# Attention feeding a soft mixture of experts on one core: small load buffers, repeated-column constants, and the last five weight halves streamed in by rows

## The chip, the cores and the metric

The kernel runs on one core of one Trainium2 chip. The metric is the device time of one execution in microseconds (us), taken as the median of three runs. One further execution was recorded by the hardware profiler; durations of single instructions come from that one.

## The reference, cut to what matters

```python
# q, k, v: (8, 12, 448, 64); phi: (768, 32); w1: (8, 768, 1024); w2: (8, 1024, 768), all float32
scores = q @ k.T / 8                                  # per batch and head
m = max(scores, -1);  e = exp(scores - m)
attn = e / (sum(e, -1) + exp(-m) + 1e-9)
x = (attn @ v) with heads side by side                # (8*448, 768)

logits = x @ phi                                      # (3584, 32): 8 experts of 4 slots
d = exp(logits - max over tokens);  d /= sum over tokens
slot_input = d.T @ x                                  # (32, 768)
h = relu(slot_input[e] @ w1[e]);  slot_out = h @ w2[e]    # per expert, its 4 slots
c = exp(logits - max over slots);  c /= sum over slots
out = c @ slot_out                                    # (3584, 768), written as float32
```

All 3584 tokens must have gone into `slot_input` before any expert can start, and all experts must be done before any output can be written.

## The kernel before, in words

The work has three stages.

**Attention.** The 96 heads are taken as 48 pairs (`NPAIR`), and three pairs make a group (`NP = 3`, 16 groups, two groups per batch). A hand-written loop over `s` from 0 to 48 sets the order of every engine. Step `s` does the second score pass (`Bk`, L298 and L300, with the exponential on ScalarE, L303) of pair `s`, the attention-times-values products (`AV`, L328) of pairs `s` and `s-1`, the transposes (`T`, L204) of pair `s+6`, and the first score pass (`A`, L226 and L235, with the row maximum on VectorE, L230 and L237) of pairs further on. The maxima of a group are negated and put in order by GpSimd (`W1`, L244), and turned by TensorE (`W2`, L264) with ScalarE's copy and exponential (`W3`). In `Bk` the matmul of L300 adds the negated maximum to the scores; its stationary operand is a slice of `sel`, a 0/1 selector whose 128 columns are equal. `N1`/`N2` normalise a pair (the GpSimd part is L353, L358, L359), `PX` (L371, L374) turns it, and once per batch the steps of `P(b)` add that batch to the running logits and `slot_input` sums; two of them use `ones` as stationary operand (L424 and L451). Five of `P(b)`'s pieces for the last batch run after the loop.

**Experts.** `hidden` (L631), `turn` (L638) and `slots` (L647) run for experts 0 to 3 and then for 4 to 7. `slots` walks over the eight rows `kt` of its four `w2` halves.

**Output.** Eight blocks, one per batch: matmul (L690), scaling on ScalarE and VectorE (L696, L698), and output DMAs from SyncE (L702, L703).

**Loads.** Every input DMA is issued by GpSimd and converts float32 to bfloat16 on its way. GpSimd's queue is in order, so the issues stand between its `N2`, `V` and `W1` work. `load(g, nm)` brings q, k or v of a group: q and k in one DMA each, v in two. `V(g)` (L309 to L312) copies v into the layout that `AV` reads. The sixteen weight halves (`halves`: `w1` of experts 0 to 7 are numbers 0 to 7, `w2` of experts 0 to 7 are numbers 8 to 15) are 1536 KB each in bfloat16. A half of `w2` has 8 rows; a row is 128 partitions of 768 numbers, 192 KB. `load_part(i, z0, z1)` brings rows `z0` to `z1` of half `i`.

**Memory.** Before, q, k and v of a group share one of two buffers of the pool `pnat`, each as large as a weight half. Ten halves have buffers of their own (`wpool`). Halves 10 and 11 take the `pnat` buffers when these are free at the end, and 12 to 15 lie over `R`, one large tile that holds attention's working buffers (`qk` for transposed pairs, `x0`/`x1` for a batch's attention output, `wm`, `vp0`/`vp1` for v, `e1`/`e2` for exponentials, `xT`). A row of a late half can be loaded when the buffers under it have been read for the last time. The last ones to come free are `xT`, which is read by the last logits matmuls (L397), and `x1`, which is read by the last `slot_input` matmuls (L451).

Of the kernel before, what the change touches and what calls it, by code (L numbers as in the profile page):

```python
# [23 lines left out]
HG = 6  # L24
NP = 3
W65 = 65
VS = 66
# [3 lines left out]
def kernel(  # L31
# [29 lines left out]
    keep = ctx.enter_context(tc.tile_pool(name="keep", bufs=1))  # L61
    pnat = ctx.enter_context(tc.tile_pool(name="pnat", bufs=2))
    wpool = ctx.enter_context(tc.tile_pool(name="wpool", bufs=10))

# [14 lines left out]

    NQK, NE, VPN = 7, 5, HG * 4 * VS  # L80
# [35 lines left out]
    w_tile = lambda: wpool.tile([128, KC * F], BF16, tag="w", name="w_sb")  # L116
    late0 = [0, KC * F, 2 * KC * F, at_["x1"]]
    for i in range(4):
        w_view(12 + i, R[:, late0[i]:late0[i] + KC * F])

    with ExitStack() as at:
# [10 lines left out]
        def load(g, nm, l0=0, l1=NP):  # L132


            b, h0 = g // 2, (g % 2) * HG
            if g not in nat:
                nat[g] = pnat.tile([128, KC * F], BF16, tag="nat", name="nat")
            z = "qkv".index(nm) * NP * S
            src = {"q": q, "k": k, "v": v}[nm][b, h0:h0 + HG]
            if nm != "v":  # L140
                t = nat[g][:, z:z + NP * S].rearrange("p (l x) -> p l x", l=NP)
                x = src.rearrange("(l h) (j t) d -> (h j) l (t d)", h=2, t=7)
                gdma(out=t[:, l0:l1, :], in_=x[:, l0:l1, :])
            else:
                t = nat[g][:, z:z + HG * 4 * D].rearrange("p (h t d) -> p h t d", h=HG, t=4)
# [19 lines left out]
        for base in (0, 64):  # L165

            nc.gpsimd.affine_select(
                out=sel[base:base + 64], in_=sel[base:base + 64], fill=1.0,
                compare_op=ALU.not_equal, base=0,
                pattern=[[-1, HG], [0, 128]], channel_multiplier=1)  # L170
        nc.vector.memset(halfm, 0.0)
# [108 lines left out]
        def Bk(n, i):  # L280
            g, pl = divmod(n, NP)
            t = qkT[n]
            rs = [slice(0, 64), slice(64, 128)]
            if i < 3:
                pss = [pb_("ps_b") for _ in range(2)]
                outs = [p[:, 0:S] for p in pss]
                cols = slice(i * 128, (i + 1) * 128)
                e = e2_t[st["e2"] % NE]
                st["e2"] += 1
                es = [e[:, hl, :] for hl in range(2)]  # L290
            else:
                pss = [pb_("ps_b")]
                outs = [pss[0][r, 0:S] for r in rs]
                cols = slice(384, 448)
                es = [e1_t]
            m = cols.stop - cols.start
            for hl in range(2):
                nc.tensor.matmul(outs[hl], t[rs[hl], 1, cols], t[rs[hl], 0, :], start=True, stop=False)  # L298
            for hl in range(2):
                nc.tensor.matmul(outs[hl], sel[rs[hl], 2 * pl + hl, 0:m], mT[mg(n)][rs[hl], :],  # L300
                                 start=False, stop=True)
# [82 lines left out]
        def P(b):  # L384
# [37 lines left out]
            def s_max():  # L422
                ps = pa([128, 128], F32, "ps_bc")
                nc.tensor.matmul(ps, ones, v["diag"], start=True, stop=True)  # L424
# [19 lines left out]
            def s_mm():  # L444
                ps = pa([128, KC + 1, NS], F32, "ps_s")
                for j in range(KC + 1):
                    for i in range(4):

                        r = slice(0, 64 if j == KC and i == 3 else 128)
                        w = x[:, i, j * 128:(j + 1) * 128] if j < KC else ones[r]  # L450
                        nc.tensor.matmul(ps[:, j, :], w, v["cd"][r, 4 + i, :], start=(i == 0), stop=(i == 3))  # L451
# [74 lines left out]
        As(1)  # L526
        for nm in "qkv":
# [80 lines left out]
        nc.vector.reduce_max(fold, ident.rearrange("p (i s) -> p s i", i=4), axis=AX.X)  # L608
# [4 lines left out]
        for g in range(2):  # L613
# [27 lines left out]
        def slots(g):  # L641
            pss = [pb_("ps_so") for _ in range(2)]
            order = list(range(FK)) if g == 0 else [4, 5, 6, 7, 0, 1, 2, 3]
            for kt in order:
                for half in range(2):
                    for i in range(4):
                        nc.tensor.matmul(pss[half][32 * i:32 * i + 32, 0:ND],  # L647
                                         hT[g][:, kt, 32 * i:32 * i + 32],
                                         w_sb["w2", 4 * g + i][:, kt, half * ND:(half + 1) * ND],
                                         start=(kt == order[0]), stop=(kt == order[-1]),  # L650
                                         skip_group_check=True)
# [82 lines left out]
```

## Time and profile before

| what | value |
|---|---|
| median of 3 runs | 344.83 us (344.19 to 344.89) |
| profiled execution, whole | 343.46 us |
| its span, first to last instruction | 341.7 us |
| mean granted TensorE clock in it | 0.936 |
| busy in the span: PE, DVE, ACT, POOL | 293.2, 264.6, 253.3, 200.2 us |
| moved by the GpSimd DMA queue | 42.52 MB, its packets taking 80.6% of 16 engines' span |
| moved by the output queue | 11.01 MB |
| read from memory, written to memory | 85.03 MB, 11.01 MB |

PE is TensorE's matmuls, PEld its weight loads (which overlap the matmuls), DVE VectorE, ACT ScalarE, POOL GpSimd, SP SyncE. A line such as L451 is a line of the kernel. In a table row, "idle before" is the time that the engine stood still ahead of those instructions, with what ended the wait behind the arrow. The three stages in this execution: attention to about 275 us, the last batch's sums and the experts to about 301 us, the output from there to the end.

### The profile page before, as it was taken

To read this page: it belongs to the slowest core of one execution; us is meant where nothing else is said; L and a number is where in the kernel's file an instruction comes from. 1 tells how busy PE (TensorE), PEld (TensorE's weight loads), DVE (VectorE), ACT (ScalarE), POOL (GpSimd) and SP (SyncE) were. 2 spreads that over 40 slices of the span, in tenths; PEclk is the share of its full clock that TensorE was granted. 3 is DMA by queue.
4 is the path that set the end of the run, shared out by engine and by line. 5 is a ranking of instruction groups with operands and counts; after the bars stand their busy time and mean duration, and the time that the engine had idled before them with its cause. 6 is when DMAs were issued, how large, how long until landed. Compare 5 with 4: busy or idle time off the path is not lost.

```text
span 341.7 us, 12065 instructions
## 1 busy us (share of the span) xinstructions
PE 293.2 (86%) x5040; PEld 167.2 (49%) x5040; DVE 264.6 (77%) x609; ACT 253.3 (74%) x547; POOL 200.2 (59%) x398
## 2 busy tenths in 40 slices
PE   3898999999999999999999999999998849677700
PEld 1344565656565655656555656565654534321100
DVE  5799999989998999898999999998984553056510
ACT  2476799998999899899989998999799823055500
POOL 8962777958687776678777867687567241000000
PEclk9999999999999999999999999999999978985555
DMA  7990999946999999199999946999919999939996
GB/s 92 126 173 0 172 169 157 197 67 87 189 169 180 134 180 138 24 142 182 161 186 136 195 56 84 156 179 194 181 28 187 154 210 211 169 89 275 338 348 238
DMA packets 42854, 54.30 MB, mean 159 GB/s; under 512 B 2736, under 2 KB 35504, under 8 KB 41904
## 3 DMA queue, kind: packets, MB, share of 16 engines
q0 software_dynamic: 41360, 42.52, 80.6%
q1 hardware_dynamic: 1440, 11.01, 9.9%
q8 instruction: 39, 0.64, 0.7%
q14 instruction: 15, 0.12, 0.1%
HBM read 85.03 MB, written 11.01 MB: 281 GB/s over the span
## 4 chain that ended last, share of the span: by engine, by line
PE 40%; DVE 25%; ACT 13%; issue 8%; DMA 5%; POOL 3%; DVEq 0%; POOLq 0%; ACTq 0%
DVE mx L230 15%; PE ps_av L328 9%; PE ps_b L298 7%; PE ps_a L226 6%; ACT R L303 6%; DMA R<-in_moe_w_dram 5%; PE ps_b L300 5%; PE ps_t L204 4%; PE ps_o L690 3%; ACT R L207 3%; ACT o_sb L696 2%; ACT R L374 2%; DVE mx L237 2%; PE ps_s L451 2%; PE ps_a L235 1%
## 5 line engine op out<-in xcount | busy, mean ns | idle before, releaser
L230 DVE TENSOR_REDUCE mx<-ps_a 128x1 f32<-128x448 f32 x288 | 160.8, 615 | 11.1 <-PE ps_a L226 9.9
L303 ACT ACTIVATE R<-ps_b 128x448 bf16<-128x448 f32 x336 | 158.0, 557 | 13.7 <-PE ps_b L300 9.1
L298 PE MATMUL ps_b<-R 64*128 64x448 bf16 (+1 forms) x384 | 82.3, 357 | 1.0 <-ACT R L374 0.3
L300 PE MATMUL ps_b<-mT,sel 64*128 64x448 bf16 (+1 forms) x384 | 78.2, 352 | 0.0
L226 PE MATMUL ps_a<-R 64*128 64x448 bf16 x288 | 68.5, 364 | 6.0 <-DVE mx L230 4.4
L353 POOL TENSOR_TENSOR R<-ubuf,rec 128x384 bf16<-128x384 f32 x44 | 36.2, 823 | 52.0 <-DVE rec L350 49.9
L328 PE MATMUL ps_av<-R 128*128 128x65 bf16 (+1 forms) x1536 | 64.5, 196 | 1.5 <-DVE ubuf L340 1.4
L328 PEld LDWEIGHTS <-R 128*128 128x128 bf16 (+1 forms) x1536 | 50.3, 100 | 28.1 <-issue 24.1
L204 PEld LDWEIGHTS <-nat 64*64 64x64 bf16 x1344 | 30.1, 113 | 18.9 <-issue 8.6
L374 ACT CAST R<-ps_x 128x512 bf16<-128x512 f32 x47 | 28.1, 598 | 13.8 <-PE ps_x L371 13.8
L204 PE MATMUL ps_t<-ident,nat 64*64 64x64 bf16 x1344 | 30.7, 196 | 7.1 <-DMA nat<-in_q_dram 4.3
L298 PEld LDWEIGHTS <-R 64*128 64x128 bf16 (+1 forms) x384 | 19.2, 97 | 27.9 <-issue 23.1
L300 PEld LDWEIGHTS <-sel 64*128 64x128 bf16 (+1 forms) x384 | 21.0, 97 | 23.1 <-issue 15.8
L237 DVE TENSOR_REDUCE mx<-ps_a 128x1 f32<-128x448 f32 x48 | 29.8, 620 | 0.8 <-PE ps_a L235 0.5
L207 ACT COPY R<-ps_t 128x896 bf16<-128x896 bf16 x20 | 18.4, 919 | 10.6 <-PE ps_t L204 10.6
L340 ACT COPY ubuf<-ps_av 128x455 f32<-128x455 f32 x44 | 24.7, 561 | 2.0 <-PE ps_av L328 1.0
L226 PEld LDWEIGHTS <-R 64*128 64x128 bf16 x288 | 17.8, 94 | 14.4 <-issue 3.6
L690 PE MATMUL ps_o<-w_sb,cT 32*128 32x384 bf16 x64 | 17.6, 456 | 5.9 <-ACT o_sb L696 5.2
L698 DVE TENSOR_SCALAR o_sb<-ps_o,crec 128x768 f32<-128x768 f32 (+1 forms) x16 | 15.5, 1009 | 9.0 <-PE ps_o L690 9.0
L696 ACT ACTIVATE o_sb<-ps_o,crec 128x768 f32<-128x768 f32 x16 | 13.5, 896 | 11.0 <-PE ps_o L690 11.0
L359 POOL TENSOR_TENSOR R<-ubuf,rec 128x128 bf16<-128x128 f32 x44 | 17.5, 398 | 3.7
L371 PE MATMUL ps_x<-ident,R 128*128 128x128 bf16 x192 | 18.8, 219 | 0.3 <-DVE R L359 0.3
(117 smaller groups left out, 371.0 us busy)
## 6 DMA issues: line engine op xcount, KB each, us to landing
w_sb<-in_moe_w_dram POOLq DMA_DIRECT2D x20, 768.0 KB, 9.6
nat<-in_v_dram POOLq DMA_DIRECT2D x32, 192.0 KB, 4.4
out_dram<-o_sb SPq DMA_DIRECT2D x7, 768.0 KB, 8.8
nat<-in_q_dram POOLq DMA_DIRECT2D x15, 336.0 KB, 5.6
nat<-in_k_dram POOLq DMA_DIRECT2D x15, 336.0 KB, 6.5
out_dram<-o_sb SPq DMA_DIRECT2D x7, 576.0 KB, 8.1
nat<-in_moe_w_dram POOLq DMA_DIRECT2D x4, 768.0 KB, 9.8
R<-in_moe_w_dram POOLq DMA_DIRECT2D x4, 384.0 KB, 12.5
```

The costliest lines, as they stand in the source:

```text
L204: nc.tensor.transpose(ps[r, a, c:c + 64], src[r, pl, tok * D:(tok + 1) * D], ident[r, r])
L207: nc.scalar.copy(t, ps)
L226: nc.tensor.matmul(pss[hl][:, 0:S], t[r, 0, i * 128:(i + 1) * 128], t[r, 1, :], start=True, stop=True)
L230: nc.vector.reduce_max(mx[g][:, c:c + 1], pss[hl][:, 0:S], axis=AX.X)
L237: nc.vector.reduce_max(mx[g][:, c:c + 1], ps[:, 0:S], axis=AX.X)
L298: nc.tensor.matmul(outs[hl], t[rs[hl], 1, cols], t[rs[hl], 0, :], start=True, stop=False)
L300: nc.tensor.matmul(outs[hl], sel[rs[hl], 2 * pl + hl, 0:m], mT[mg(n)][rs[hl], :], start=False, stop=True)
L303: nc.scalar.activation(e, p[:, 0:S], AF.Exp, scale=scale)
L328: nc.tensor.matmul(o, eT[n, i, hl][:, qc], vp[g % 2][:, 2 * pl + hl, i, 0:W65], start=(i == 0 and u == 0 and hl == 0), stop=(i == 3), skip ...
L353: eng.tensor_mul(x[:, 0:3, c:c + 128].rearrange("p i (h d) -> p i h d", h=2), u[:, 0:6, 0:D].rearrange("p (i h) d -> p i h d", h=2), rec[: ...
L374: nc.scalar.copy(xT[:, pb, :], ps)
L690: nc.tensor.matmul(pss[i][0:m, half, 0:ND], cT[r, b, 0:m], slot_out[r, half * ND:(half + 1) * ND], start=True, stop=True)
```

## The change

- q, k and v get small buffers inside `R`: `nq0` and `nq1` (q and k of even and odd groups) and one `nv` for v. The pool `pnat` is gone. `R` is ordered anew.
- Because there is one `nv`, v of group `g` is issued right behind `V(g-1)`, in the step where `s` is a multiple of 3, and ahead of q and k of the group after it. Before, it was issued one step later, behind `W1`, and one group further ahead.
- `sel` is one column per head and `ones` one column; the matmuls read them as 128 (or 64) repeated columns, with a step of zero.
- Eleven halves have buffers of their own. They start at steps 1, 4, 7, 10, 13, 16, 22, 25, 28, 31 and 34 (each half in two parts, in that step and the next).
- Halves 11 to 15 lie over `R` from its start, and are loaded by rows from step 38 on.
- `slots` takes its rows in the order 0 to 7 for both expert groups. Before, the second group took 4 to 7 first.

```diff
-    pnat = ctx.enter_context(tc.tile_pool(name="pnat", bufs=2))
-    wpool = ctx.enter_context(tc.tile_pool(name="wpool", bufs=10))
+    wpool = ctx.enter_context(tc.tile_pool(name="wpool", bufs=11))
...
-    ones = const.tile([128, 128], BF16, name="ones")
-    sel = const.tile([128, HG, 128], BF16, name="sel")
+    ones = const.tile([128, 1], BF16, name="ones")
+    sel = const.tile([128, HG], BF16, name="sel")
...
-    sizes = [("qk", NQK * 2 * S), ("x0", 4 * DD), ("wm", 2 * 512), ("vp0", VPN), ("e1", S),
-             ("e2", NE * 2 * S), ("vp1", VPN), ("x1", 4 * DD), ("xT", KC * 512)]
+    sizes = [("nq0", 2 * NP * S), ("nq1", 2 * NP * S), ("nv", NATV), ("wm", 2 * 512),
+             ("qk", NQK * 2 * S), ("vp0", VPN), ("x0", 4 * DD), ("e2", NE * 2 * S), ("e1", S), ("vp1", VPN),
+             ("xT", KC * 512), ("x1", 4 * DD)]
...
-    late0 = [0, KC * F, 2 * KC * F, at_["x1"]]
-    for i in range(4):
-        w_view(12 + i, R[:, late0[i]:late0[i] + KC * F])
+    for i in range(5):
+        w_view(11 + i, R[:, i * KC * F:(i + 1) * KC * F])
...
-                nc.tensor.matmul(outs[hl], sel[rs[hl], 2 * pl + hl, 0:m], mT[mg(n)][rs[hl], :],
+                nc.tensor.matmul(outs[hl], sel[rs[hl], 2 * pl + hl:2 * pl + hl + 1].to_broadcast([64, m]), mT[mg(n)][rs[hl], :],
...
-        half_at = {s: i for i, s in enumerate((1, 4, 10, 13, 16, 22, 25, 28, 34, 37))}
-
-        part_at = {44: ((12, 0, 2), (12, 7, 8)), 45: ((12, 2, 3),), 46: ((12, 3, 4), (13, 0, 7)), 47: ((12, 4, 5),)}
+        half_at = {s: i for i, s in enumerate((1, 4, 7, 10, 13, 16, 22, 25, 28, 31, 34))}
+
+        part_at = {38: ((11, 0, 3),), 41: ((11, 3, 7),), 42: ((11, 7, 8), (12, 0, 1)), 44: ((12, 1, 5),),
+                   45: ((12, 5, 7), (13, 2, 4)), 46: ((12, 7, 8), (13, 4, 8)), 47: ((13, 0, 2), (14, 0, 1))}
...
                 V(g - 2)
+                if s and g - 1 < NG:
+                    load(g - 1, "v")
...
-                if g < NG:
-                    load(g, "v")
+                if s == 1:
+                    load(2, "v")
...
-            if s in (39, 42):
-                i = 10 + (s - 39) // 3
-                load_half(i, 0, pnat.tile([128, KC * F], BF16, tag="nat", name="nat"))
-                load_half(i, 1)
...
-        load_part(12, 5, 7)
-        load_part(13, 7, 8)
-        load_part(14, 0, 8)
+        load_part(14, 1, 8)
+        load_part(15, 0, 1)
...
-        load_part(15, 4, 8)
-        load_part(15, 0, 2)
-        load_part(15, 2, 4)
+        load_part(15, 1, 5)
+        load_part(15, 5, 8)
...
-            order = list(range(FK)) if g == 0 else [4, 5, 6, 7, 0, 1, 2, 3]
-            for kt in order:
+            for kt in range(FK):
```

More of the change, by code (lines that the diff above doesn't have):

```diff
@@ L72 @@
     ident2 = const.tile([128, 128], BF16, name="ident2")
[L73 to L74 removed]
+    ones = const.tile([128, 1], BF16, name="ones")
+    sel = const.tile([128, HG], BF16, name="sel")
     phi_sb = const.tile([128, KC, NS], BF16, name="phi_sb")
     halfm = const.tile([128, 2], F32, name="halfm")
[L80 to L82 removed]
+    NQK, NE, VPN, NATV = 7, 5, HG * 4 * VS, HG * 4 * D
+    sizes = [("nq0", 2 * NP * S), ("nq1", 2 * NP * S), ("nv", NATV), ("wm", 2 * 512),
+             ("qk", NQK * 2 * S), ("vp0", VPN), ("x0", 4 * DD), ("e2", NE * 2 * S), ("e1", S), ("vp1", VPN),
+             ("xT", KC * 512), ("x1", 4 * DD)]
     at_, n_ = {}, 0
@@ L135, in load @@
             b, h0 = g // 2, (g % 2) * HG
-            if g not in nat:
-                nat[g] = pnat.tile([128, KC * F], BF16, tag="nat", name="nat")
-            z = "qkv".index(nm) * NP * S
             src = {"q": q, "k": k, "v": v}[nm][b, h0:h0 + HG]
             if nm != "v":
-                t = nat[g][:, z:z + NP * S].rearrange("p (l x) -> p l x", l=NP)
+                t = part(f"nq{g % 2}", "qk".index(nm) * NP * S, NP * S).rearrange("p (l x) -> p l x", l=NP)
                 x = src.rearrange("(l h) (j t) d -> (h j) l (t d)", h=2, t=7)
@@ L144, in load @@
             else:
-                t = nat[g][:, z:z + HG * 4 * D].rearrange("p (h t d) -> p h t d", h=HG, t=4)
+                t = part("nv", 0, NATV).rearrange("p (h t d) -> p h t d", h=HG, t=4)
                 x = src.rearrange("h (p t) d -> p h t d", t=7)
@@ L169 @@
                 compare_op=ALU.not_equal, base=0,
-                pattern=[[-1, HG], [0, 128]], channel_multiplier=1)
+                pattern=[[-1, HG]], channel_multiplier=1)
         nc.vector.memset(halfm, 0.0)
@@ L423, in s_max @@
                 ps = pa([128, 128], F32, "ps_bc")
-                nc.tensor.matmul(ps, ones, v["diag"], start=True, stop=True)
+                nc.tensor.matmul(ps, ones.to_broadcast([128, 128]), v["diag"], start=True, stop=True)
                 nc.vector.reduce_max(new, ps.rearrange("p (i s) -> p s i", i=4), axis=AX.X)
@@ L449, in s_mm @@
                         r = slice(0, 64 if j == KC and i == 3 else 128)
-                        w = x[:, i, j * 128:(j + 1) * 128] if j < KC else ones[r]
+                        w = x[:, i, j * 128:(j + 1) * 128] if j < KC else ones[r].to_broadcast([r.stop, 128])
                         nc.tensor.matmul(ps[:, j, :], w, v["cd"][r, 4 + i, :], start=(i == 0), stop=(i == 3))
@@ L526 @@
         As(1)
-        for nm in "qkv":
+        for nm in "qk":
             load(2, nm)
-        half_at = {s: i for i, s in enumerate((1, 4, 10, 13, 16, 22, 25, 28, 34, 37))}
-        part_at = {44: ((12, 0, 2), (12, 7, 8)), 45: ((12, 2, 3),), 46: ((12, 3, 4), (13, 0, 7)), 47: ((12, 4, 5),)}
+        half_at = {s: i for i, s in enumerate((1, 4, 7, 10, 13, 16, 22, 25, 28, 31, 34))}
+        part_at = {38: ((11, 0, 3),), 41: ((11, 3, 7),), 42: ((11, 7, 8), (12, 0, 1)), 44: ((12, 1, 5),),
+                   45: ((12, 5, 7), (13, 2, 4)), 46: ((12, 7, 8), (13, 4, 8)), 47: ((13, 0, 2), (14, 0, 1))}
         for s in range(NPAIR + 1):
@@ L649, in slots @@
                                          w_sb["w2", 4 * g + i][:, kt, half * ND:(half + 1) * ND],
-                                         start=(kt == order[0]), stop=(kt == order[-1]),
+                                         start=(kt == 0), stop=(kt == FK - 1),
                                          skip_group_check=True)
```

## The prediction

> **What bounds the kernel now.** I read the page first, then the chain of waits at its end, then a table of stretches, then the timelines of single engines around the edits. The chain says what set the end:
>
> ```profile
> 281.74 0.70 POOL R L107
> 282.44 16.09 DMA R<-in_moe_w_dram
> 298.56 0.66 PE ps_so L647 x9
> 299.25 0.49 ACT w_sb L652
> ```
>
> Columns are start, us, what. A weight DMA issued at 282.44 lands 16.09 us later, and the second `slots` waits for it. A DMA issued into an empty queue lands far sooner, so this one stood behind others. The timeline of PE shows the three waits (1.73, 0.38 and 1.02 us, 3.1 together):
>
> ```profile
> 294.84 1.48 PE L647 MATMUL ps_so<-R,w_sb 128*32 128x384 bf16 x32 [1.73 <-DMA R<-in_moe_w_dram]
> ...
> 296.71 0.83 PE L647 MATMUL ps_so<-R,w_sb 128*32 128x384 bf16 x16 [0.38 <-DMA R<-in_moe_w_dram]
> ...
> 298.56 0.81 PE L647 MATMUL ps_so<-R,w_sb 128*32 128x384 bf16 x13 [1.02 <-DMA R<-in_moe_w_dram]
> ```
>
> The table of stretches (columns: stretch, its length, busy PE, PEld, DVE, ACT, POOL with counts, granted clock, DMA share, GB/s) shows when the queue was free and when full:
>
> ```profile
> 200.00:205.00 5.00, 5.00 (x91) 2.91 (x92) 4.43 (x11) 4.52 (x11) 2.92 (x6) 1.00 0.02 5
> ...
> 250.00:255.00 5.00, 5.00 (x78) 2.79 (x75) 4.83 (x12) 4.91 (x12) 3.58 (x8) 1.00 0.02 4
> ...
> 290.00:295.00 5.00, 3.10 (x71) 1.85 (x75) 1.27 (x3) 0.48 (x1) 0.00 (x0) 1.00 1.16 210
> ...
> 310.00:315.00 5.00, 3.82 (x14) 1.06 (x14) 2.81 (x3) 2.60 (x4) 0.00 (x0) 0.50 1.02 265
> ```
>
> DMA idles at 200 and 250 and is full from about 262 to 298: the last weights are late because too many were left for the end. Attention itself is near full on PE, DVE and ACT together, so it shortens only where a wait goes. The output is full on DMA from 310 on (a block of 1.38 MB takes 3.9 us at about 350 GB/s, its compute 3.13 us in the chain), so it starts when `slots` ends and keeps its length, whatever the clock of 0.50.
>
> **The tail.** Two last rows are 384 KB, and the last two waits end 298.56 - 296.71 = 1.85 us apart: 0.93 us a row. Page part 6 agrees (1536 KB issued at 274.87 lands after 16.1, 768 KB issued at 277.84 after 17.0: 3.8 us for four). Before, 40 rows (halves 11 to 15) are issued from 254.82 on. After, seven rows of half 11 go at steps 38 and 41 (about 232 and 248.5), where DMA has room, two at step 42, and 31 from 262.44 on, where the first late part is issued now. An empty queue needs 3.4 to 4.0 us from issue to first transfer (four rows issued at 254.82 land after 7.8; seven issued at 269.24 after 10.0). So the 31 start at 265.8 to 266.4 and, at 0.94, land at 295.0 to 295.6. They do not starve, as every part is issued before the queue reaches it: `(12,5,7)` and `(13,2,4)` at about 263 (`Bk(45)` ends 262.8), `(12,7,8)` at 267 (`Bk(46)` ends 266.9), `(13,4,8)` at 269.2 (the wait for L451 is there now), `(13,0,2)` at 272.5, half 14 at 274.9, the last two at 277.8 and 281.7.
>
> The last DMA brings rows 5 to 7 of half 15, which `slots` now takes last. From the last landing to the eviction (L652) two rows take 0.69 us (298.56 to 299.25), three 0.69 + 0.33 = 1.02. The eviction moves from 299.25 to 296.0 to 296.6: 2.6 to 3.2 us gained, I take 2.9. Ceiling: the first `slots` needs 2.67 us from start to eviction (290.17 to 292.84); the second without a wait would evict at 295.5, a gain of 3.75. Floor: rows land 1.0 us apart while attention runs (192 KB parts between 268 and 271); 31 at that rate end at 297.2, a gain of 0.95.
>
> **GpSimd at 252 to 259.** Here the chain runs over POOL: `V(15)`, two 768 KB issues of 1.58 us, `N2`, `W1`, and PE waits 0.22 + 0.21 us for `W1`. The two issues become single rows, and four issues of 192 or 384 KB took 2.41 us, 0.60 each. That frees 0.4 us; I take 0.3 (bounds 0 and 0.43).
>
> **Start.** The memset of `ones` (0.17 us on DVE, on the chain at 6.94) becomes one like L178's 0.07: 0.1 gained. `sel` cost POOL 0.82 + 1.78 us and falls to about 0.7 (by L255's 0.12 and the `ident` select's 0.29), but `W1(0)` behind it waits for L237 until 11.62, and PE is in `T(2)` until 12.64. I take nothing for that.
>
> **v ahead of q and k, on POOL.** In steps divisible by 3 two v issues (1.4 us) now stand ahead of `N2` and `W1`:
>
> ```profile
> 94.82 0.76 POOL L143 DMA_DIRECT2D nat<-in_k_dram  x1
> 95.65 0.82 POOL L353 TENSOR_TENSOR R<-ubuf,rec 128x384 bf16<-128x384 f32 x1
> ...
> 97.20 0.85 POOL L244 TENSOR_SCALAR R<-mx 128x36 bf16<-128x36 f32 x3
> 98.13 0.28 POOL L244 TENSOR_SCALAR ngm<-mx 128x21 bf16<-128x21 f32 x1
> ```
>
> In such a group `N2` follows with no idle time, so it slips 1.4. `W1`'s three operands for PE end at 98.05 and PE starts `W2` at 99.50: 1.45 us of cover, just enough. In the groups between, POOL idles 1.27 us before `N2`. I take 0; if that cover is gone, 0.2 us in each of seven groups, 1.4. The step-1 issues and the weight parts keep their number.
>
> **v ahead of q and k, in the DMA queue.** The queue is in order, so k lands up to 2.05 us later (two v parts land 1.0 apart). Slack today: k issued at 48.69 lands after 6.6, at 55.3, and `T(12)` starts on PE at 57.15: 1.85. `T(15)` likewise 1.85. Worst is k issued at 223.48, landing after 9.3, at 232.8, with `T(45)` at 233.38: 0.6. Elsewhere 2.2 to 4.6. Full slips would cost 0.2 + 0.2 + 1.45 = 1.85. But the weight parts no longer queue behind v and so finish sooner. I take 0.4 lost (bounds 0 and 1.85). The extra half at step 7 and that at step 31 use the idle DMA time around 70 to 78 and 201 to 206: nothing.
>
> **Repeated columns.** 384 loads of `sel` and, by five a batch, 40 of `ones` now read one column 64 or 128 times. No load of the trace has step zero. Loads are pipelined: twelve of 128 columns take 0.42 us (L328), 35 ns each, and a pair of `sel` loads 0.11, inside the 0.19 us that the pair of matmuls before it takes.
>
> ```profile
> 16.05 0.12 PEld L300 LDWEIGHTS <-sel 64*128 64x128 bf16 x2
> ...
> 21.83 0.42 PEld L328 LDWEIGHTS <-R 128*128 128x128 bf16 x12
> ```
>
> Nothing gets shorter, since the same instructions are there. The upper bound is the slowest mean of a load on the page, 113 ns (L204), not overlapped: 0.226 a pair, 0.036 too long in 192 pairs, 6.9 us. I take 0, by the nearest row (L328). [...]
>
> **Sum.** Against the profiled execution's 343.46: -2.9 - 0.3 - 0.1 + 0.4 = -2.9, so 340.6. The median of the runs is 1.37 higher, 344.83; from there 341.9.
>
> **Rivals.** (1) Slower: loads at step zero are not fast. Decides from a pair of 0.205 us on (0.19 + 2.9/192): at 113 ns a load and with half of the 6.9 to all of it seen, 345.4 to 348.8, say 347. For it: no row shows such a load, and L300 sits on the chain in every step. Against it: a load may become three times slower than L328's 35 ns before anything waits. (2) A weak gain: the rows come at 1.0 us each or k is late by the full 1.85, 342.7 to 344.1, say 343.4. For it: the 0.6 us of slack at `T(45)`; against it: queue and cover as counted. (3) It does nothing: the 31 rows starve behind a wait and the last still lands near 298.5, 344.8. Against it: the issue times above.
>
> **Chances.** Forecast 0.74 (340.6 to 343.0, by the tail's ceiling and floor), weak gain 0.11, nothing 0.03, slower 0.12. The range 340.5 to 344.2 takes in the first two and leaves out the slow case, some of the third and a little below. What can be told from no change is 0.2%, 0.7 us: faster 0.80 (a part of the weak gain is within it), same 0.05, slower 0.15 (the slow case, and late loads that add to a missed tail).
>
> **What would show it.** Right: L647 waits for DMA for under 1.2 us in all, the eviction L652 comes 2.5 to 3.2 us earlier, DMA is busy at 200 to 206, and the stretch from the last L652 to the end stays at 42.4 us. `sel` loads stay near 97 ns and L300 at 352. Wrong: L300's pairs over 0.2 us; PE waiting for q or k at `T` in many groups; L264 waiting for POOL; the last DMA still landing 16 us after its issue.

## The result, and the profile after

The changed kernel takes 341.96 us (median of four runs, 340.57 to 342.29) beside 344.51 us for the kernel before on the same chip (343.74 to 344.89). The ratio is 0.9925, with a 95% interval of 0.9897 to 0.9953: about 2.5 us faster, with 341.9 predicted. A second set, of six runs, gave 341.55, ratio 0.9894 (0.9863 to 0.9925).

The total came as predicted, the way to it did not, and the profile of the changed kernel shows it at once. Its profiled execution took 341.64 us (span 339.9, mean granted clock 0.929), 1.82 less than the 343.46 of before. The line numbers have moved: `slots` is now L639, its evictions L644 and L645, `hidden` L624, the last `slot_input` matmuls L447, `T` L200, `W2` L260.

The end of the chain of waits (start, us, what), where the chain of before had a DMA of 16.09 us:

```profile
281.61 1.03 PE ps_s L447 x28
283.07 7.94 PE ps_h L624 x50
291.98 0.70 DVE w_sb L632
292.73 5.25 PE ps_so L639 x124
298.00 0.49 ACT w_sb L644
```

There is no DMA in it. `slots` (L639) runs through both expert groups without a stop, and what now sets the end is TensorE itself. The three waits of 3.1 us are gone, as the group of the second `slots` says (busy, mean ns of one, and idle time before, which is zero):

```profile
L639 PE MATMUL ps_so<-R,w_sb 128*32 128x384 bf16 x80 | 5.4, 326 | 0.0
```

Yet the eviction came only 1.25 us earlier, at 298.00 instead of 299.25. The table of stretches shows where the rest went (stretch, length, busy PE, PEld, DVE, ACT, POOL with counts, granted clock, DMA share, GB/s):

```profile
260.00:265.00 5.00, 4.35 (x65) 2.29 (x64) 3.48 (x13) 4.54 (x13) 3.43 (x6) 1.00 0.16 9
...
270.00:275.00 5.00, 4.88 (x89) 2.91 (x89) 2.93 (x12) 4.24 (x9) 1.99 (x3) 1.00 1.16 209
...
280.00:285.00 5.00, 3.17 (x49) 1.70 (x52) 2.67 (x11) 0.74 (x3) 0.77 (x1) 0.50 1.16 210
285.00:290.00 5.00, 5.00 (x68) 1.97 (x64) 0.00 (x0) 1.59 (x3) 0.00 (x0) 0.67 1.16 210
290.00:295.00 5.00, 4.49 (x93) 2.74 (x89) 1.99 (x6) 1.16 (x2) 0.00 (x0) 1.00 1.09 197
```

Three of the same stretches of before:

```profile
270.00:275.00 5.00, 4.65 (x89) 2.95 (x87) 3.12 (x13) 3.93 (x10) 2.19 (x5) 1.00 0.95 146
...
280.00:285.00 5.00, 3.87 (x64) 2.05 (x67) 2.15 (x9) 1.10 (x4) 1.41 (x2) 0.59 1.15 207
285.00:290.00 5.00, 4.66 (x85) 2.38 (x73) 1.27 (x5) 2.38 (x4) 0.00 (x0) 1.00 1.16 210
```

Two things are to be seen. The queue never runs below 1.05 from 265 to 295 after; before, it was at 0.95 and 146 GB/s from 270 to 275. And TensorE's clock was granted at half speed for longer: 0.50 and 0.67 in the two stretches from 280, where before had 0.59 and 1.00. `hidden`, 96 matmuls, took 7.94 us instead of 6.31. Its row of before:

```profile
282.15 6.31 PE L631 MATMUL ps_h<-w_sb,ubuf 128*32 128x512 bf16 x96 [0.45 <-DVE ubuf L472]
```

The prediction read the queue of before as full from about 262 to 298; the row of 270 to 275 shows that it was not. GpSimd had issued five rows (four DMAs) from 262.44 on and then stood in a wait for L451:

```profile
262.44 2.41 POOL L107 DMA_DIRECT2D R<-in_moe_w_dram  x4
269.24 1.55 POOL L107 DMA_DIRECT2D R<-in_moe_w_dram  x2 [4.38 <-PE ps_s L451]
```

The last of the five rows landed at 271.28, and the seven rows issued at 269.24 had landed only at 279.21. At the 209 GB/s of the changed kernel the stretch from 270 to 275 would have moved 0.32 MB more: 1.6 rows, or an estimated 1.5 us.

A ledger of the two profiled executions, by when the same instruction starts after and before:

| up to | after minus before, us | what happened on the way |
|---|---|---|
| `T` at about 21.5 | +0.28 | full clock granted a little later (from 18.69 instead of 17.88) |
| `T(12)` | +0.35 more | PE waits 0.39 for k |
| `T(45)` | +0.34 more | PE waits 0.34 for k |
| `W2` at 259 | -0.38 | no more wait for GpSimd |
| L447 at 281.61 (L451 at 280.69) | +0.92 in all | +0.33 in many small steps |
| end of `hidden` and `turn` | +2.5 in all | half clock for longer |
| eviction L644 (L652) | -1.25 in all | the 3.1 us of waits and some 0.7 of restarts behind them gone |
| end | -1.8 in all | output stage 41.9 instead of 42.4 |

The first three entries, from the timeline of PE after (before, the second group started at 21.27 and the others did not wait):

```profile
11.67 0.96 PE L200 MATMUL ps_t<-ident,R 64*64 64x64 bf16 x28 [0.23 <-DVE mx L233]
...
21.55 0.63 PE L200 MATMUL ps_t<-ident,R 64*64 64x64 bf16 x28 [0.19 <-DVE mx L233]
...
58.20 0.41 PE L200 MATMUL ps_t<-ident,R 64*64 64x64 bf16 x14 [0.39 <-DMA R<-in_k_dram]
...
234.56 0.41 PE L200 MATMUL ps_t<-ident,R 64*64 64x64 bf16 x14 [0.34 <-DMA R<-in_k_dram]
```

The same 28 transposes take 0.96 us at 11.67 and 0.63 at 21.55. The first clock record of this trace, full speed, begins between the two, at 18.69. That instant differs from profile to profile, 17.8 to 24.1 us after the start (last section). An effect of under 1 us is therefore read below from a later instruction on.

### The profile page after: what moved, and what is told of

It reads as the page before. It is cut to its first block, busy times and chain, and to the rows that moved or that the text cites. A ratio compares the mean times of both kernels' runs of the same rounds, so it can differ in the third digit from the quotient of the medians.

```text
span 339.9 us, 12092 instructions
## 1 busy us (share of the span) xinstructions
PE 295.1 (87%) x5040; PEld 167.7 (49%) x5040; DVE 264.6 (78%) x609; ACT 253.5 (75%) x547; POOL 198.8 (58%) x399
## 4 chain that ended last, share of the span: by engine, by line
PE 43%; DVE 25%; ACT 12%; issue 6%; DMA 6%; POOL 3%; DVEq 0%; POOLq 0%; ACTq 0%
DVE mx L226 15%; PE ps_av L324 8%; PE ps_b L294 6%; PE ps_a L222 6%; DMA R<-in_k_dram 5%; ACT R L299 5%; PE ps_t L200 5%; PE ps_b L296 4%; PE ps_o L682 3%; ACT R L203 2%; PE ps_h L624 2%; ACT o_sb L688 2%; PE ps_s L447 2%; DVE mx L233 2%; ACT R L370 2%
## 5 line engine op out<-in xcount | busy, mean ns | idle before, releaser
L296 PE MATMUL ps_b<-mT,sel 64*128 64x448 bf16 (+1 forms) x384 | 78.2, 352 | 0.0
L200 PEld LDWEIGHTS <-R 64*64 64x64 bf16 x1344 | 30.3, 113 | 19.9 <-issue 8.6
L200 PE MATMUL ps_t<-ident,R 64*64 64x64 bf16 x1344 | 31.2, 196 | 7.9 <-DMA R<-in_q_dram 4.3
L296 PEld LDWEIGHTS <-sel 64*128 64x128 bf16 (+1 forms) x384 | 21.1, 97 | 23.1 <-issue 15.6
L222 PEld LDWEIGHTS <-R 64*128 64x128 bf16 x288 | 17.8, 94 | 14.6 <-issue 3.8
```

The costliest lines, as they stand in the source:

```text
L200: nc.tensor.transpose(ps[r, a, c:c + 64], src[r, pl, tok * D:(tok + 1) * D], ident[r, r])
L222: nc.tensor.matmul(pss[hl][:, 0:S], t[r, 0, i * 128:(i + 1) * 128], t[r, 1, :], start=True, stop=True)
L296: nc.tensor.matmul(outs[hl], sel[rs[hl], 2 * pl + hl:2 * pl + hl + 1].to_broadcast([64, m]), mT[mg(n)][rs[hl], :], start=False, stop=True)
```

## The experiments

The theory after this reading: the gain is the tail of weight rows, the half clock took part of it, the repeated columns cost nothing and the order of v, q and k costs 0.7 us. The rivals were that the rows of half 11 that go early are the gain (the prediction's reason), that the clock and not the DMA is the bound, and that the columns matter. Each ratio is to the kernel before on the same chip. Not all of these kernels ran on the chip of the base, so from one heading to another the ratios are to be compared, not the times.

### The changed kernel again, as the base

> The changed kernel itself, on the chip on which its variants run. Expected against the kernel before: ratio 0.990 to 0.995 (before 344.5 us, this 341 to 342.5). In its profile the second slots does not wait for a weight DMA, hidden runs partly at half clock (in the profile before 96 matmuls of hidden take 6.3 us, in the profile after 7.9), and PE waits about 0.35 us each for k at the transposes of pairs 12 and 45.

341.55 us (339.87 to 342.72), ratio 0.9894 (0.9863 to 0.9925). Again no wait in `slots`; `hidden` again took 7.9 us, with the half clock from 277.5 to 287.7; the last row landed at 295.78 and the eviction came at 297.45. One expectation failed: `T(12)` and `T(45)` did not wait for k. One wait of 0.23 us came at `T(36)` instead:

```profile
185.92 0.41 PE L200 MATMUL ps_t<-ident,R 64*64 64x64 bf16 x14 [0.23 <-DMA R<-in_k_dram]
```

So the two waits of the first profile, 0.39 and 0.34 us, are no fixed price of the new order. The section on q and k takes this up.

### The repeated columns alone, in the kernel before

```diff
-    ones = const.tile([128, 128], BF16, name="ones")
-    sel = const.tile([128, HG, 128], BF16, name="sel")
+    ones = const.tile([128, 1], BF16, name="ones")
+    sel = const.tile([128, HG], BF16, name="sel")
...
-                nc.tensor.matmul(outs[hl], sel[rs[hl], 2 * pl + hl, 0:m], mT[mg(n)][rs[hl], :],
+                nc.tensor.matmul(outs[hl], sel[rs[hl], 2 * pl + hl:2 * pl + hl + 1].to_broadcast([64, m]), mT[mg(n)][rs[hl], :],
...
-                nc.tensor.matmul(ps, ones, v["diag"], start=True, stop=True)
+                nc.tensor.matmul(ps, ones.to_broadcast([128, 128]), v["diag"], start=True, stop=True)
...
```

> The kernel before with one part of the change alone: sel and ones as single columns, read with a step of zero. Theory (a load with step zero is as fast as any): a pair of sel loads stays at about 0.11 us, L300's matmuls at 352 ns, and the time is that of the kernel before within 0.3 us (344.5 to 345.1). Rival (such loads are slower and cost up to 6.9 us, which something else in the change gives back): 346 or more.

344.46 beside 344.57, ratio 0.9987 (0.9961 to 1.0012). The timeline of PEld and the groups of this kernel:

```profile
16.18 0.12 PEld L300 LDWEIGHTS <-sel 64*128 64x128 bf16 x2
```

```profile
L300 PE MATMUL ps_b<-mT,sel 64*128 64x448 bf16 (+1 forms) x384 | 78.2, 352 | 0.0
L300 PEld LDWEIGHTS <-sel 64*128 64x128 bf16 (+1 forms) x384 | 21.0, 97 | 23.1 <-issue 15.8
```

A pair of loads takes the 0.12 us it took before, the mean load 97 ns, and L300's matmuls 352 ns without idle time. Here a weight load with a step of zero is as fast as one with a step of one.

### All of half 11 late again

```diff
-        part_at = {38: ((11, 0, 3),), 41: ((11, 3, 7),), 42: ((11, 7, 8), (12, 0, 1)), 44: ((12, 1, 5),),
+        part_at = {42: ((11, 0, 4), (11, 4, 8), (12, 0, 1)), 44: ((12, 1, 5),),
```

> The changed kernel with half 11 loaded whole at step 42 instead of seven rows of it at steps 38 and 41. Theory of the prediction taken by its number of rows (seven rows more in the tail, 0.94 us each, 6.6 us): the last landing moves from 296.4 to about 300 or later and the kernel is 2 to 4 us slower than the changed one, near the kernel before (344 to 345). Rival (memory, not the number of rows, holds the queue: it stands idle from 260.2 to about 266 in the profile after, and the nine rows of step 42 fit into that): the last landing moves by under 1 us, still ahead of its matmuls, and the time is that of the changed kernel within 0.4 us (342.0 to 342.3).

341.34 (340.78 to 342.85), ratio 0.9896 (0.9868 to 0.9925), beside 341.55 for the base: no difference, though seven rows more, 1.3 MB, are issued from step 42 on. The last row landed at 296.11. Its stretches:

```profile
260.00:265.00 5.00, 4.55 (x62) 2.10 (x60) 3.89 (x13) 4.60 (x13) 3.67 (x6) 1.00 1.15 208
265.00:270.00 5.00, 4.09 (x80) 2.65 (x80) 2.89 (x10) 3.61 (x10) 1.02 (x3) 1.00 1.17 210
270.00:275.00 5.00, 4.88 (x93) 2.98 (x89) 2.83 (x11) 4.07 (x9) 1.54 (x3) 1.00 1.15 208
```

In the changed kernel the queue stands nearly idle from 260 to 265 (0.16, 9 GB/s), because nothing is issued between 256.42 and 263.01. Here the seven rows use just that hole (1.15, 208 GB/s), and from about 267 on the same 31 rows follow. So the early rows only moved a hole; they are not the gain. This kernel issues as many rows late as the kernel before, 40: it needs 41.5 us from the first issue (254.57) to the last landing, where the kernel before needed 43.7 (254.82 to 298.52). The prediction's reason falls, and the other difference in the tail, that the queue does not run dry later, is what remains. The next experiment takes that away.

### Five rows issued behind the wait for L447

In the changed kernel nine rows (`(12,1,5)`, `(12,5,7)`, `(13,2,4)`, `(12,7,8)`) lie over buffers that come free before `x0`, and GpSimd issues them before it waits for L447, the reader of `x0`. Before, the rows issued from 262.44 on that could go ahead of the corresponding wait were five. This kernel changes nothing but the order of issue:

```diff
-                   45: ((12, 5, 7), (13, 2, 4)), 46: ((12, 7, 8), (13, 4, 8)), 47: ((13, 0, 2), (14, 0, 1))}
+                   46: ((13, 4, 8), (12, 5, 7), (13, 2, 4), (12, 7, 8)), 47: ((13, 0, 2), (14, 0, 1))}
```

> The changed kernel with five rows (two of half 12, two of half 13, one of half 12) issued behind the part that waits for the last-but-one batch's slot_input sums, instead of ahead of it. Theory (the gain comes from a queue that never runs dry between 262 and 296, because the new order of buffers lets nine rows go ahead of that wait, and not from fewer rows): the queue stands for 3 to 3.5 us after its first four rows, the last landing moves from 295.8 to about 299, and most of the gain is lost: 343.5 to 344.2. Rival (TensorE sets the end, the queue has room): within 0.4 us of the changed kernel, 341.5 to 342.

344.81, ratio 1.0017 (0.9993 to 1.004): the whole gain is lost. The timeline of GpSimd shows the gap between the issues, the stretches the queue, and the timeline of PE the waits that are back:

```profile
263.09 0.82 POOL L107 DMA_DIRECT2D R<-in_moe_w_dram  x1
270.10 2.72 POOL L107 DMA_DIRECT2D R<-in_moe_w_dram  x4 [6.20 <-PE ps_s L447]
```

```profile
265.00:270.00 5.00, 4.09 (x77) 2.40 (x74) 2.70 (x10) 3.99 (x10) 0.00 (x0) 1.00 0.86 153
270.00:275.00 5.00, 4.88 (x88) 2.91 (x87) 2.94 (x11) 4.24 (x9) 3.97 (x6) 1.00 0.74 107
```

```profile
296.60 1.48 PE L639 MATMUL ps_so<-R,w_sb 128*32 128x384 bf16 x32 [2.17 <-DMA R<-in_moe_w_dram]
299.41 1.14 PE L639 MATMUL ps_so<-R,w_sb 128*32 128x384 bf16 x21 [1.33 <-DMA R<-in_moe_w_dram]
```

Four rows keep the queue busy for less than four microseconds, the next issue comes 7 us after the first, at 270.10, and the queue runs dry: nothing lands between 269.76 and 277.10, when the first four rows of that issue do. The last row lands at 299.37 and 3.5 us of waits return. The same number of rows, with the same buffers, is then as slow as before.

The gap here is longer than that of the kernel before: from 265 to 275 the queue moved 0.65 MB less than in the first profile of the changed kernel (153 and 107 GB/s beside 182 and 209), an estimated 3.1 us of rows, where the kernel before lost an estimated 1.5. So this run shows that such a wait alone can take the whole gain, not that the gap of before was all of the 2.2 us by which half 11 late again was quicker. A part of the rest lies in the rate: the last 20 rows took 0.97 us each before (279.21 to 298.52), the last 22 of half 11 late again 0.94 (275.41 to 296.11). Why the rate differs is not shown.

In the first profile of the changed kernel the same issues stand as follows:

```profile
263.01 2.25 POOL L107 DMA_DIRECT2D R<-in_moe_w_dram  x3
267.84 0.55 POOL L107 DMA_DIRECT2D R<-in_moe_w_dram  x1 [2.58 <-PE ps_b L296]
270.01 0.74 POOL L107 DMA_DIRECT2D R<-in_moe_w_dram  x1 [1.62 <-PE ps_s L447]
```

### q and k first, v behind them

```diff
                 V(g - 2)
-                if s and g - 1 < NG:
-                    load(g - 1, "v")
             if s == 1 or (s and s % 3 == 0):
                 if g < NG:
                     load(g, "q")
                     load(g, "k")
+            if s and s % 3 == 0 and g - 1 < NG:
+                load(g - 1, "v")
```

> The changed kernel with q and k of the next group issued ahead of v instead of behind it. Theory (v ahead of q and k delays k): the two waits for k at the transposes of pairs 12 and 45, 0.39 and 0.34 us, go, v has 16 us to spare, so attention ends 0.6 us earlier and the kernel is 0.6 us faster than the changed one (341.3 where that has 341.9). Rival (PE's waits there are made up later, VectorE or ScalarE being the bound): waits go, end of attention and time unchanged within 0.2 us.

340.66 (339.56 to 341.53), ratio 0.9869 (0.9837 to 0.9901), beside 341.55: 0.9 us better in the median, with intervals that overlap. No `T` waits for k: `T(45)`, which a wait split in the first profile of the changed kernel, runs in one piece, and so does `T(36)`, which one split in the base.

```profile
233.44 0.60 PE L200 MATMUL ps_t<-ident,R 64*64 64x64 bf16 x28
```

One pair of profiles would not settle this, as the waits move. But all six profiles with v first have one or two of them after the start: 0.39 at `T(12)` and 0.34 at `T(45)` in the first, 0.23 at `T(36)` in the base, 0.43 at `T(12)` with half 11 late, 0.63 at `T(36)` with five rows behind the wait, 0.28 at `T(33)` with the last rows first and 0.74 at `T(27)` with TensorE kept busy. None of the eight others has one, three of the kernel before or its variants and five with q and k first. The last `slot_input` matmuls (L447) start at 280.67, 0.47 us earlier than in the base, although full clock came 0.36 us later.

In this execution the half clock lasted only 6.8 us, and at once the DMA is late again by a little (idle time 0.6):

```profile
L639 PE MATMUL ps_so<-R,w_sb 128*32 128x384 bf16 x80 | 5.7, 326 | 0.6 <-DMA R<-in_moe_w_dram 0.6
```

### Last rows first, the old order of `slots`

```diff
-            for kt in range(FK):
+            order = list(range(FK)) if g == 0 else [5, 6, 7, 0, 1, 2, 3, 4]
+            for kt in order:
...
```

> The changed kernel with the second slots taking rows 5, 6, 7 ahead of 0 to 4, so that it needs the last DMA at once. Theory (the last landing at 296.4 has only some 0.9 us to spare against the matmuls that need it at 297.3): the second slots now stands from 295.4 to 296.4 and the kernel is about 1.1 us slower than the changed one (343.0). Rival (the last landing has several us to spare and TensorE alone sets the end): no difference, within 0.3 us.

342.29 (341.57 to 343.98), ratio 0.9929 (0.9902 to 0.9957), beside 341.55: 0.7 worse in the median, intervals overlapping. The last DMA brings rows 5 to 7, and the second `slots` can do almost nothing before it has landed:

```profile
296.99 2.76 PE L640 MATMUL ps_so<-R,w_sb 128*32 128x384 bf16 x61 [2.00 <-DMA R<-in_moe_w_dram]
```

Of its 64 matmuls 61 come behind the last landing, 2.63 us up to the eviction at 299.62, where three rows would take about 1.05. So the order can be worth up to 1.6 us, by this estimate, once the DMA is the bound; the medians show 0.7 and do not settle it. This profiled execution lies 1.3 us above the kernel's median: its full clock came only at about 23.4 us, and `T(45)` starts 1.2 us later than in the base.

### TensorE kept busy, after and before

Fourteen added matmuls, whose product nothing uses, stand in the gaps of the last batch's sums; the expectation counts twelve. The same edit was made in the changed kernel and in the kernel before.

```diff
+        def warm(n):
+            for _ in range(n):
+                nc.tensor.matmul(wps[0], ident, w_sb["w1", 7][:, 0, 0:512], start=True, stop=True)
...
+        warm(2)
         last[1]()
+        warm(1)
         PX(NPAIR - 1)
...
-                    both(lambda: l_mm([PB - 1]), l_ev, l_turn, s_max, d_sub, lambda: exps(4, 8), corr,
-                         s_mm, s_last, c_max, c_sub, lambda: exps(0, 4)),
+                    both(lambda: warm(1), lambda: l_mm([PB - 1]), l_ev, lambda: warm(2), l_turn, lambda: warm(2), s_max, d_sub,
+                         lambda: warm(5), lambda: exps(4, 8), corr, s_mm, lambda: warm(1), s_last, c_max, c_sub, lambda: exps(0, 4)),
```

> The changed kernel with twelve added matmuls (448 to 512 columns, their result unused) in TensorE's waiting times between the last attention step and hidden. Theory (the half clock from about 277.5 on comes from TensorE standing still there, and costs hidden up to 1.7 us): the half-clock stretch of 6.8 or 10.2 us goes or is shorter, hidden takes about 5.5 us, and then the last weight DMA (landing at 295.8) sets the end of the second slots again, so the kernel is only 0.3 to 0.7 us faster than the changed one (340.9 to 341.3). Rival (the added matmuls only lie in the way): the clock stays as it is and the time rises by 0.3 us or more.

After: 341.76 (339.56 to 343.03), ratio 0.9914 (0.9885 to 0.9942). The clock stayed full and `hidden` fell to 5.4 us, but the time did not move, where 0.3 to 0.7 us were expected:

```profile
280.00:285.00 5.00, 4.58 (x75) 2.41 (x77) 2.67 (x11) 1.34 (x4) 0.77 (x1) 1.00 1.15 209
```

```profile
293.57 1.49 PE L649 MATMUL ps_so<-R,w_sb 128*32 128x384 bf16 x32 [0.38 <-DMA R<-in_moe_w_dram]
296.39 1.14 PE L649 MATMUL ps_so<-R,w_sb 128*32 128x384 bf16 x21 [1.33 <-DMA R<-in_moe_w_dram]
```

The 2.5 us won in `hidden` turned into 1.7 us of waiting for the last rows (last landing 296.34), with the eviction at 297.39. In the changed kernel two limits lie within about a microsecond of each other: the last landing at full clock, TensorE at half clock. Taking away either leaves the other. The ten executions of the changed kernel on record say the same. Five have a mean clock of 0.928 or 0.929, as the two profiles with 10.2 us at half clock, and a median of 341.4 us; five have 0.935 or 0.936, as profiles with 6.8 us, and a median of 342.1. A longer half clock is not seen in the time, so it can't be said to have cost the change a part of its gain.

> The kernel before with fourteen added matmuls (their result unused) in TensorE's waiting times between the last attention step and hidden. Theory (before, the last weight landing alone set the end, TensorE being ahead of it): the half clock goes and hidden ends about 1 us earlier, the wait for weights in the second slots grows by as much, and the time is that of the kernel before within 0.4 us. Rival (the half clock cost the kernel before time as well): 0.8 to 1.2 us faster than the kernel before.

Before: 344.23, ratio 0.9996 (0.9976 to 1.0016). `hidden` and its transposes' start came 1.3 us earlier (287.17 instead of 288.46) and the second `slots` only waited longer, in one piece:

```profile
295.27 5.28 PE L657 MATMUL ps_so<-R,w_sb 128*32 128x384 bf16 x61 [3.44 <-DMA R<-in_moe_w_dram]
```

So before the change the last landing alone was the bound, as the prediction read the chain. In this execution the granted clock fell during the wait of 3.4 us: it is 0.94 from 290 to 295 and 0.50 from 295 to 300, for the matmuls behind it.

### All three at once, and what went wrong with it

This kernel put q and k first, added the matmuls, and issued rows 1 to 4 of half 12 one step earlier:

```diff
-        part_at = {38: ((11, 0, 3),), 41: ((11, 3, 7),), 42: ((11, 7, 8), (12, 0, 1)), 44: ((12, 1, 5),),
+        part_at = {38: ((11, 0, 3),), 41: ((11, 3, 7),), 42: ((11, 7, 8), (12, 0, 1)), 43: ((12, 1, 5),),
...
```

> The changed kernel with three edits: q and k issued ahead of v, rows 1 to 4 of half 12 issued one step earlier (step 43, when their memory is free and the queue stands idle), and the twelve added matmuls. Theory (two bounds lie close together at the end, the last weight landing and TensorE at half clock, and both must move): the last landing comes 2 us earlier, at about 293.5, hidden takes 5.5 us, the second slots ends at about 294.5 to 295, and the kernel is 2.5 to 3 us faster than the changed one (338.5 to 339.1). Rival (the output stage gives it back): under 1.2 us faster, no better than q and k first alone (340.4 to 340.7).

353.4, ratio 1.0254 (1.0218 to 1.0291). The edit was a mistake, and the run is a result on waits only. Row 1 lies over the slot of `wm` with the maxima of pairs 45 to 47, and row 4 over the slot of `qk` that pair 44 still uses, so the scores of pair 44 and the maxima of the next three pairs are then made from weights. The chain shows how the load came into the middle of attention:

```profile
260.50 6.88 DMA R<-in_moe_w_dram
...
267.43 0.56 PE ps_b L294 x2
```

`Bk(44)` waited 11 us for a weight load. It tested neither theory. In the next two only rows 2 and 3 of half 12, which lie over free buffers, go at step 43, first with the added matmuls and then without them.

> The changed kernel with q and k issued ahead of v, rows 2 and 3 of half 12 (the two whose memory is no longer used then) issued at step 43 instead of 44, and fourteen added matmuls with unused result. Theory (two bounds lie close together at the end and both must move): no half clock before 300, the last weights land at about 292.5 to 293.5, the second slots does not wait and its eviction starts at 294.8 to 295.3 (297.4 in the changed kernel on this chip), 2.0 to 2.6 us faster than the changed kernel, 339.0 to 339.6. Rival (the output stage or the added matmuls give it back): no better than q and k first alone, 340.5 or more.

341.03 (339.56 to 341.96), ratio 0.9893 (0.9862 to 0.9924). The gain expected beyond q and k first is missing: the rows issued behind the wait for L447 at 270.73 landed only at 279.70, 6.4 us after the landing ahead of them, where four rows take 3.7. `slots` waited 1.3 us again, and the last row landed at 296.59, where 292.5 to 293.5 was expected.

> The same without the added matmuls: q and k ahead of v, and rows 2 and 3 of half 12 at step 43. Theory: the weights land at about 293, the second slots never waits, and TensorE at half clock for 6.8 or 10.2 us sets the end: eviction at 295.7 to 297, 0.9 to 1.7 us faster than the changed kernel, 339.9 to 340.7, so 0.5 to 1.3 us slower than with the added matmuls. Rival (the half clock does not matter once the weights are early): the same time as with them, within 0.3 us.

340.77 (340.15 to 342.11), ratio 0.9890 (0.9857 to 0.9923): no wait in `slots`, half clock 6.8 us, last landing at 296.16 instead of the expected 293, eviction at 297.21. The rival held: the time is that of the kernel with the added matmuls within 0.3 us. Neither differs from q and k first alone. Rows issued earlier into the hole at 260 leave fewer for later: from 265 to 275 the queue moved 175 and 179 GB/s in the first of the two kernels and 132 and 200 in the second, where the base has 203 and 207.

### Matmuls at the start

Ten matmuls over a zeroed buffer, eight before `T(0)` and two behind it, with q and k first, against the slower clock at the start (28 transposes in 0.96 us at 11.67, in 0.63 at 21.55).

```diff
+        nc.vector.memset(ubuf.rearrange("p n c -> p (n c)").bitcast(BF16)[:, 0:512], 0.0)
...
+        warm(8)
         T(0)
+        warm(2)
         As(2)
```

> The changed kernel with q and k issued ahead of v, and ten added matmuls of 512 columns with unused result at the start: eight from about 0.7 us on, when TensorE waits for the first load until 4.3, and two behind the first transposes. Theory (the clock is granted in full only after a stretch of steady work, from 17.8 to 24.1 us on by the execution, and the work till then runs at half clock): the full clock comes earlier, at 14 us or before, attention ends 0.8 to 1.5 us earlier and the kernel is at 339.2 to 339.9, the best so far (340.7 without the added matmuls). Rival (the start of the full clock does not depend on these, or VectorE alone sets the pace there): within 0.3 us of the kernel without them.

341.05 (339.44 to 341.67), ratio 0.9903 (0.9875 to 0.993): nothing gained over q and k first (0.9869). The clock did rise early, at 6.5 us, and fell back at 9.9 (28 transposes take 0.95 us at 4.72, 0.63 at 8.28 and 0.95 at 11.21); it came for good at 23.6 us, within the range of the other profiles:

```profile
8.00:12.00 4.00, 3.22 (x63) 1.95 (x62) 3.86 (x8) 0.91 (x1) 2.19 (x9) 0.74 1.23 161
12.00:16.00 4.00, 3.81 (x25) 1.22 (x21) 2.76 (x6) 2.53 (x6) 3.85 (x9) 0.50 1.15 142
```

The fastest version of the study is the changed kernel with q and k first, 340.66 us; that it beats the changed kernel is likely from the waits for k that it removes, but not settled by the times, whose intervals overlap.

## Why the prediction was right, and where it was not

- **What bounds the kernel**: right. With more TensorE clock and nothing else, the kernel before did not get faster; it only waited longer for the last rows.
- **The tail, -2.9**: the reason given was wrong, and the size too large in the profiles. The last landing moved by 2.1 us, from 298.52 to 296.44, where 295.0 to 295.6 was predicted; the 31 rows took about 0.97 us each instead of 0.94 and were issued 0.57 later (263.01). The argument "seven rows fewer" is wrong: with them late again the time is the same. It rests on the reading that the queue of before was full from 262 to 298, and from 270 to 275 it was not. Before, 40 rows at 0.94 from 258.6 (issue at 254.82 and 3.8 to the first transfer) would by this estimate have been done at 296.2; the kernel with half 11 late again, whose queue does not run dry, landed its 40 at 296.11. The sentence "they do not starve", written as a check on a rival, was the actual mechanism. The nine rows ahead of the `x0` wait are what the new order of buffers gave.
- **The eviction at 296.0 to 296.6**: missed, 298.00. The step that failed took TensorE's side of the ceiling, 295.5, from the profile of before as if it were fixed. It became 298.0, as attention ended 0.9 later and `hidden` took 1.6 longer at half clock. TensorE at half clock evicts between 297.2 and 298.0 in the profiles without a wait in `slots`, so once the DMA was no longer late, TensorE was. The miss is 1.4 to 2.0 us in this execution, and most of it is the landing: with 1.05 us behind it, as with TensorE kept busy, 296.44 gives an eviction at 297.5. The last 0.5 us are TensorE's.
- **GpSimd at 252 to 259, -0.3**: right; the step at `W2` is -0.38 and the waits of 0.22 and 0.21 are gone.
- **Start, -0.1**: not seen. The clock's own spread, 0.28 in this pair, covers it.
- **v ahead on GpSimd, 0**: right. In the groups after, L260 has no idle time and L261 0.1 us in all.
- **v ahead in the queue, +0.4**: `T(12)` and `T(45)` waited in the first profile, and `T(15)` in none. The waits make 0.2 to 0.7 us by profile, around the 0.4 taken and inside the bounds. But they also came at `T(27)`, `T(33)` and `T(36)`, where the prediction saw 2.2 to 4.6 us of slack; with q and k first there are none.
- **Repeated columns, 0**: right, shown alone.
- **The output stage unchanged at 42.4**: 41.9 here, and 41.7 to 42.5 over all profiles, with or without the change. The -0.5 lies within that spread.
- **The rivals**: the slow loads did not exist (a pair of `sel` loads takes 0.12 us). Starvation, put at 0.03, did not happen, but it is a real price: 2.9 us in the profiled executions (344.27 beside 341.36) when five rows move behind one wait. The weak gain, 1.4 us, is what the pair of profiled executions comes nearer to, with 1.82; the medians of the two sets say 2.55 and 3.30.
- **The interval 340.6 to 343.0**: it does not follow from the tail's ceiling and floor. With -3.75 and -0.95 in place of -2.9 the same sum gives 341.1 and 343.9.

Of the signs named for being right, three came: no wait in `slots`, DMA busy from 200 to 205 (1.13), and `sel` loads at 97 ns with L296 (L300 before) at 352. The output stage stayed within its spread. The eviction 2.5 to 3.2 us earlier did not come.

That 341.9 met 341.96 has luck in it. For the profiled execution 340.6 was predicted and 341.64 came, 1.0 too much; the step from there to the median was taken as 1.37, as before, and was 0.32. The two misses cancel.

## What to carry to other kernels

When loads of the last stage wait for buffers to come free, count not how many are left but whether the queue holds enough ahead of every wait of the issuing engine: in these runs four rows of 0.94 us did not bridge a 7 us gap, nine did. Place in memory what comes free first so that its loads go ahead of the longest wait. Before pricing the removal of a DMA wait, work out when the waiting engine itself would be done, and at the lower clock that a pause just ahead of it can leave (here 0.50 and 0.67 in the two stretches from 280).

## What the runs showed of the hardware

- The granted clock falls to half where TensorE pauses for the last batch's sums: in the profile after it is busy 2.20 of the 5 us from 275 to 280, and the clock is 0.81 there and 0.50 from 280 to 285. In the changed kernel with the added matmuls it is busy 3.85 of these 5 us, and the clock stays at 1.00. The half clock lasts 6.8 or 10.2 us by execution: whole steps of 3.4 (before 6.83, from 277.29; after 10.24, from 278.11; the full clock that follows lasts 20.48 and 13.65, six and four such steps). `hidden` took 5.4 us (never at half), 6.3 to 6.9 or 7.8 to 7.9 us. Which of the two lengths comes can be read from the ten profiles with half clock there. It was two steps where the last L447 (L451 before) began by the end of the first step (before: half clock from 277.29, so 280.70, and L451 at 280.69), three where it began later (changed kernel: from 278.11, so 281.52, and L447 at 281.61; base: from 277.46, so 280.87, and 281.14). So by these profiles the longer half clock is a matter of where the steps fall in an execution. In the kernel before with the added matmuls the clock fell in a DMA wait of 3.4 us as well (0.50 from 295 to 300). At the start, where TensorE had short pauses, full clock came 17.8 to 24.1 us after the first instruction by the records, while TensorE was busy 3.81 of the 4 us from 12 to 16 (profile after). Ten added matmuls brought it to 6.5 us, and it fell back at 9.9. What sets this moment is not shown.
- Where full clock came later, the work behind it came later too: `T(6)` at 29.98 with full clock from 17.88 (before), at 30.26 from 18.69 (after), at 31.41 from about 23.4 (last rows first). Over the profiles `T(6)` starts at 29.94 to 31.74, up to 1.8 us apart, beside a spread of some 2 to 3 us between runs of one kernel. That the start of full clock is the cause of most of that spread is likely, not shown. An effect below 1 us has to be read from the profile, from a later instruction on.
- From issue to landing an empty queue needed an estimated 2.3 to 4.0 us ahead of the rows' own time of 0.94 us each (one row issued at 255.36 in the base landed after 3.27, four issued at 254.82 before after 7.76). In the kernel with rows 2 and 3 at step 43 and the added matmuls it was once 5.2 (four rows issued at 270.73 landed after 8.96, the row ahead of them at 273.30). With five rows behind the wait for L447, where the queue had run dry, it was 3.2 by the same estimate (four rows issued at 270.10 landed at 277.10).
